# Raw queries and keys in a ring of five half buffers, and a 28th resident weight quarter

## The chip, the cores and the metric

The kernel runs on one core of a Trainium2 chip. The metric is the device time of one launch in microseconds (us), the median of several runs. Five engines work side by side: TensorE (PE, with its weight loads as PEld), VectorE (DVE), ScalarE (ACT), GpSimd (POOL) and SyncE (SP). SP issues all DMA transfers of this kernel, in one order written out in the program.

## What is computed

Attention with a decay for 8 batches of 8 heads (576 positions, 64 channels), and on its result a soft mixture of 8 experts:

```python
scores = scale * np.matmul(q, k.transpose(0, 1, 3, 2))
cum = np.cumsum(np.log(np.clip(f, 0.0001, 1.0)), axis=-1)
scores = np.where(causal, -1000000000.0, scores + cum[:, :, :, None] - cum[:, :, None, :])
attn = softmax(scores)                    # 64 heads, 576 x 576
x = (attn @ v)                            # then as 4608 x 512
logits = x @ phi                          # 32 slots, 4 for each expert
slot_input = softmax(logits, over tokens).T @ x
h = relu(slot_input[e] @ w1[e]); slot_out[e] = h @ w2[e]     # 8 experts, 512 x 1024 and 1024 x 512
out = softmax(logits, over slots) @ slot_out
```

## The kernel before

The 64 heads are worked off in 32 pairs; `g` is a pair, `h0 = 2g` and `h1 = 2g+1` are its heads. One pass of the loop over `g` (L699 on) does for pair `g` the scores (`s2`, L262), their exponentials (`expo`, on ACT, L282), the causal blanking (`causal`, on POOL: one L290 and two L293 for a head), and the product with the values (`s3`, 25 matmuls of the program for a head, L310). For the pairs ahead it does the score maxima (`s1` on PE, `tops` on DVE); those of pair `g+1` are turned into a row and sent with a small DMA (`mrows`, `YA<-mr`, L260), for which the first `s2` of the next pass waits. The values of a head are normed by `norm` on DVE (L325 to L330), and the normed tiles `X` are turned on PE by `px` (L337), for the logits of the experts.

Queries and keys come as fp32 (`load_qk`, `RAW<-in_qk`, L166: both heads of a pair in one transfer of 576 KB) and are split into two parts. ACT rounds them (`round_k` L175 into `WA`, `round_q` L180 into `YA`). Two DMAs on SP copy the rounded parts to the other half of the partitions (`dup_q` L195, `YB<-YA`, and `dup_k` L191, `WB<-WA`, 288 KB each for a pair). POOL subtracts the rounded from the raw: `low_k(i)` (L201) reads raw keys and the copy in `WB`, `low_q(i)` (L206) raw queries and `YA`. So a raw buffer is free when ACT has rounded and POOL has subtracted. There are three of them, `RAW[0]` to `RAW[2]`, one for a pair.

The expert weights are 64 quarters of 512 KB. In the loop, passes 4 to 30 each load one into a tile of its own (`wload`, `w<-in_w`, L120): 27 resident ones. The others go into tiles that the attention leaves (`wstream`): `RAW[2]`, then `RAW[0]` and two tiles `p2` at the end of pass 29, `RAW[1]`, `p0` and three `p1` at the end of pass 30, later `PTS`, `V`, `X`, and at last 20 of the resident tiles again. After the loop come the last logits, the two expert layers (`mlp1`, L907, and `mlp2`, L945) and the output in blocks (L1018, L1019), staged in the three raw buffers, `p2` and `p0`.

Nothing is scheduled by a planner: each engine does its instructions in the order of the program, and waits in place where an operand is not ready. The order in which each `s3` reads the columns of the probabilities `PT` is fixed by `VALUES` (L66): the 8th and the 9th of its 25 matmuls are the first that read columns which L293 blanks.

Of the kernel before, what the change touches and what calls it, by code (L numbers as in the profile page):

```python
# [7 lines left out]
F32 = mybir.dt.float32  # L8
# [19 lines left out]
TOP = (97, 66, 66)  # L28
NRES = 27
NQ = 8 * NE  # L30
QW = 1024
DEFER = 4
# [36 lines left out]
def attn_softmoe(ctx: ExitStack, tc: tile.TileContext, qk, v, f, phi, w1, w2, cst, out):  # L69
# [23 lines left out]
    for n, m in enumerate((1, 0, 2)):  # L93
        YA[m] = fr[n].tile([P, 2, 640], F32R, name=f"YA{m}")
        WA[m] = fr[n].tile([P, 2 * S], F32R, name=f"WA{m}")
        if m < 2:
            YB[m] = fr[n].tile([P, 2, S], F32R, name=f"YB{m}")
            WB[m] = fr[n].tile([P, 2 * S], F32R, name=f"WB{m}")
    RAW = [per.tile([P, 2, S], F32, name=f"RAW{i}") for i in range(3)]
    PTS = per.tile([P, 3200], F32, name="PTS")  # L100
    PT = [PTS[:, 1600 * i : 1600 * i + 1600] for i in range(2)]
    X = [per.tile([P, NBLK, 256], F32, name=f"X{i}") for i in range(3)]
    XT = [per.tile([P, S], F32, name=f"XT{i}") for i in range(NPAIR)]
    V = per.tile([P, 2, NBLK, 130], F32, name="V")
    EX = per.tile([P, 256], F32, name="EX")
    LD = const.tile([P, NBLK, NS], F32, name="LD")

    LG = const.tile([P, 256], F32, name="LG")
    fin = const.tile([P, 8], F32, name="fin")
# [36 lines left out]
    def pair(g):  # L146
        return 0 <= g < NG
# [14 lines left out]

    def load_qk(g):
        if pair(g) and ("r", g) not in st:
            st["r", g] = RAW[g % 3]
            nc.sync.dma_start(RAW[g % 3], qk[g])  # L166

    def load_v(g):
        if pair(g):
            nc.sync.dma_start(V[:, g % 2], v[g])  # L170

    def round_k(g, *hs):
        if pair(g):
            for h in hs or range(2):
                nc.scalar.copy(WA[g % 3][0:64, S * h : S * h + S], RAW[g % 3][64:128, h])  # L175

    def round_q(g, *hs):
        if pair(g):
            for h in hs or range(2):
                nc.scalar.copy(YA[g % 3][0:64, h, 64:640], RAW[g % 3][0:64, h])  # L180

# [11 lines left out]
    def dup_q(g, h0=0, h1=2):  # L193
        if pair(g):
            nc.sync.dma_start(YB[g % 2][0:64, h0:h1].bitcast(F32), YA[g % 3][0:64, h0:h1, 64:640].bitcast(F32))  # L195

    def low_k(i):
        if head(i):
            g, h = divmod(i, 2)
            t = WB[g % 2][:, S * h : S * h + S]  # L200
            nc.gpsimd.tensor_tensor(t[0:64], RAW[g % 3][64:128, h], t[64:128].bitcast(F32), op=ALU.subtract)  # L201

    def low_q(i):
        if head(i):
            g, h = divmod(i, 2)
            nc.gpsimd.tensor_tensor(YB[g % 2][64:128, h], RAW[g % 3][0:64, h], YA[g % 3][0:64, h, 64:640].bitcast(F32), op=ALU.subtract)  # L206

# [893 lines left out]
```

## Time and profile before

| | |
|---|---|
| median of 3 runs | 393.2 us (392.66 to 393.69) |
| profiled execution, own time | 395.0 us |
| its span (first to last instruction) | 393.2 us |
| TensorE busy | 372.6 us, 95% of the span |
| VectorE, ScalarE, GpSimd busy | 280.5, 260.1, 252.4 us |
| granted TensorE clock, mean | 0.985 |

Times in all rows are counted from the span's start. In a timeline row, the first number is the start and the second the duration, in us, of `xN` instructions in a row; in brackets stands the idle time before them and what ended it, where there was some. TensorE's records are finer than the program: a head's 25 matmuls of `s3` are 50 records. SP's rows are the issues of DMAs; the data moves later.

### The profile page before, as it was taken

What the parts mean: (1) busy time and instruction counts of PE and PEld (TensorE: products, weight loads), DVE (VectorE), ACT (ScalarE), POOL (GpSimd) and SP (SyncE); (2) the same over time, 40 slices, a digit from 0 to 9 for tenths busy, and PEclk for the clock granted to TensorE, in tenths of its full rate; (3) what the DMA queues carried; (4) which work ended last, traced back from release to release, by engine and by line L of the source; (5) the groups of instructions that cost most, each with busy time, mean ns of one, the idle gap of its engine ahead of it and who ended that gap; (6) DMA issues with size and microseconds to landing.
All of it is one profiled execution on the core that took longest, in us unless ns stands there. A gap on an engine that the chain in (4) does not pass through costs nothing.

```text
span 393.2 us, 15013 instructions
## 1 busy us (share of the span) xinstructions
PE 372.6 (95%) x5827; PEld 329.7 (84%) x5827; DVE 280.5 (71%) x1074; ACT 260.1 (66%) x664; POOL 252.4 (64%) x349
## 2 busy tenths in 40 slices
PE   7999999999999999999999999999999989999860
PEld 7889999999999999999999999999999986544630
DVE  7878887878787877797879787878787534441770
ACT  8859776867786778676868686868686552021650
POOL 4797887878787878787878787878787821100000
PEclk9999999999999999999999999999999999999995
DMA  6865768677867777777777777777777989999798
GB/s 205 214 157 160 219 170 275 190 221 211 240 190 230 212 215 210 215 204 217 210 213 212 210 212 211 212 213 211 211 215 205 306 291 330 390 408 370 262 364 320
DMA packets 34343, 93.71 MB, mean 238 GB/s; under 512 B 4266, under 2 KB 8288, under 8 KB 34272
## 3 DMA queue, kind: packets, MB, share of 16 engines
q1 hardware_dynamic: 34272, 92.75, 76.1%
q8 instruction: 46, 0.75, 0.8%
q14 instruction: 25, 0.20, 0.2%
HBM read 63.93 MB, written 9.73 MB: 187 GB/s over the span
## 4 chain that ended last, share of the span: by engine, by line
PE 83%; DMA 10%; DVE 2%; ACT 2%; issue 1%; DVEq 0%; SPq 0%; ACTq 0%
PE pv L310 25%; PE ring L275 14%; PE s L222 13%; PE ring L276 13%; DMA w<-in_w 6%; PE pv L337 4%; PE lg L373 3%; DMA out<-RAW 2%; PE more L907 2%; PE ds L457 2%; DMA YA<-mr 1%; PE ring L493 1%; PE pv L248 1%; DMA PTS<-in_f 1%; ACT PTS L282 1%
## 5 line engine op out<-in xcount | busy, mean ns | idle before, releaser
L282 ACT ACTIVATE PTS<-ring 128x320 f32<-128x320 f32 (+2 forms) x256 | 119.8, 513 | 65.3 <-PE ring L276 39.2
L275 PE MATMUL ring<-YA,WA 67*128 67x320 f32 (+9 forms) x384 | 121.9, 330 | 1.2 <-DMA YA<-mr 1.2
L238 DVE CUSTOM_DVE_ANT_0 s<-s,mask 128x320 f32<-128x320 f32 (+3 forms) x256 | 109.1, 442 | 5.4 <-PE s L222 0.9
L276 PE MATMUL ring<-YB,WB 128*128 128x320 f32 (+4 forms) x384 | 110.7, 296 | 0.0
L310 PE MATMUL pv<-V,PTS 128*64 128x65 f32 x3200 | 104.3, 223 | 0.7 <-ACT mr L257 0.7
L310 PEld LDWEIGHTS pv<-V,PTS 128*64 128x64 f32 x3200 | 99.6, 137 | 3.4 <-ACT mr L257 1.2
L222 PE MATMUL s<-WA,YA 66*128 66x288 f32 (+9 forms) x384 | 98.5, 312 | 0.5 <-ACT YA L180 0.2
L201 POOL TENSOR_TENSOR WB<-RAW,WB 64x576 fp32r<-64x576 f32 x64 | 90.3, 1411 | 11.2 <-ACT YA L180 5.3
L206 POOL TENSOR_TENSOR YB<-RAW,YA 64x576 fp32r<-64x576 f32 x64 | 89.5, 1417 | 2.5
L275 PEld LDWEIGHTS ring<-YA,WA 67*128 67x128 f32 (+3 forms) x384 | 69.7, 183 | 6.9 <-issue 2.1
L276 PEld LDWEIGHTS ring<-YB,WB 128*128 128x128 f32 (+1 forms) x384 | 69.9, 182 | 0.0
L222 PEld LDWEIGHTS s<-WA,YA 66*128 66x128 f32 (+1 forms) x384 | 62.9, 190 | 7.1 <-ACT PTS L282 1.4
L293 POOL TENSOR_SCALAR_AFFINE_SELECT PTS<-PTS 128x128 f32<-128x128 f32 (+1 forms) x128 | 31.3, 265 | 25.7 <-ACT PTS L282 23.8
L238 DVE DVE_READ_ACCUMULATOR2_ANT MT<- 128x1 f32 x310 | 44.1, 142 | 0.0
L290 POOL TENSOR_SCALAR_AFFINE_SELECT PTS<-PTS 128x384 f32<-128x384 f32 x64 | 33.3, 520 | 15.6 <-ACT PTS L282 11.7
L337 PE MATMUL pv<-cs,X 128*128 128x128 f32 x155 | 42.0, 276 | 0.0
L238 DVE CUSTOM_DVE_ANT_0 s<-s,mask,MT 128x288 f32<-128x288 f32 x62 | 32.6, 526 | 11.4 <-PE s L222 2.4
L175 ACT CAST WA<-RAW 64x576 fp32r<-64x576 f32 x64 | 40.1, 669 | 0.9
L180 ACT CAST YA<-RAW 64x576 fp32r<-64x576 f32 x63 | 39.5, 670 | 0.4
L325 DVE TENSOR_SCALAR rl<-pv 128x5 f32<-128x5 f32 x64 | 10.5, 164 | 35.9 <-PE pv L310 35.3
L330 DVE TENSOR_TENSOR X<-pv,rl 128x320 f32<-128x320 f32 (+1 forms) x65 | 31.5, 486 | 2.4 <-DMA w<-in_w 0.3
L361 ACT COPY XT<-pv 128x128 f32<-128x128 f32 (+1 forms) x124 | 28.6, 292 | 0.0
(210 smaller groups left out, 371.7 us busy)
## 6 DMA issues: line engine op xcount, KB each, us to landing
w<-in_w SPq DMA_DIRECT2D x47, 512.0 KB
RAW<-in_qk SPq DMA_DIRECT2D x31, 576.0 KB
V<-in_v SPq DMA_DIRECT2D x32, 325.0 KB
YB<-YA SPq DMA_DIRECT2D x30, 288.0 KB
WB<-WA SPq DMA_DIRECT2D x30, 288.0 KB
p<-in_w SPq DMA_DIRECT2D x6, 512.0 KB
out<-RAW SPq DMA_DIRECT2D x6, 512.0 KB
out<-p SPq DMA_DIRECT2D x5, 512.0 KB
```

The lines of the kernel that those rows point to most:

```text
L175: nc.scalar.copy(WA[g % 3][0:64, S * h : S * h + S], RAW[g % 3][64:128, h])
L180: nc.scalar.copy(YA[g % 3][0:64, h, 64:640], RAW[g % 3][0:64, h])
L201: nc.gpsimd.tensor_tensor(t[0:64], RAW[g % 3][64:128, h], t[64:128].bitcast(F32), op=ALU.subtract)
L206: nc.gpsimd.tensor_tensor(YB[g % 2][64:128, h], RAW[g % 3][0:64, h], YA[g % 3][0:64, h, 64:640].bitcast(F32), op=ALU.subtract)
L222: nc.tensor.matmul(t[:, o : o + w], ya[0:m, h, 128 * blk : 128 * blk + 128], wa[0:m, j0 : j0 + w], start=True, stop=True)
L238: nc.vector.tensor_tensor_reduce(out=t[:, o : o + w], in0=t[:, o : o + w], in1=mask[:, m0 : m0 + w], scale=1.0, scalar=top if n == 3 else ...
L275: nc.tensor.matmul(o, wa[0:m, j0 : j0 + n], ya[0:m, h, 64 + i0 : 64 + i0 + w], start=True, stop=False)
L276: nc.tensor.matmul(o, wb[:, j0 : j0 + n], yb[:, h, i0 : i0 + w], start=False, stop=True)
L282: nc.scalar.activation(PT[i % 2][:, SEG_O[bank] : SEG_O[bank] + at], t[:, 0:at], AF.Exp, scale=0.125)
L290: nc.gpsimd.affine_select(d3, d3, pattern=[[0, 3], [1, 128]], compare_op=ALU.is_ge, fill=0.0, base=0, channel_multiplier=-1)
L310: nc.tensor.matmul(o[64 * u : 64 * u + 64, t, :], PT[i % 2][:, at : at + 64], V[:, g % 2, c, 65 * h : 65 * h + 65], start=(c == 0), stop=( ...
L337: nc.tensor.transpose(pm[:, 0:128], x[:, t, 128 * (p % 2) : 128 * (p % 2) + 128], ident)
```

## The change

- The raw queries and keys stand in one tile of five half buffers, one for a head: `raw(i)` is half `i % 5`. `load_qk(g, h)` loads one head (288 KB), so a pair takes two transfers, and the second of pair `g+3` goes into the half of head `h0+2`.
- In each pass POOL does `low_q(h0+2)` and `low_k(h0+2)` at the start, `low_q(h1+2)` after `causal(h0)`, and `low_k(h1+2)` at the end as before. Before, both `low_q` stood at the start and `low_k(h0+2)` after `causal(h0)`. SP issues the first half load before the value load, the second behind it and then the resident quarter.
- `dup_k` is issued ahead of `dup_q` in the loop.
- 28 resident quarters: one in each of the passes 4 to 28, and a second one in passes 18, 22 and 26 (`TWICE`); none in 29 to 31.
- Of the raw tile two pieces are taken for streamed quarters: the first behind both `p2` at the end of pass 29, the second behind `p0` and `p1` at the end of pass 30. The load at the end of pass 28 is gone. The third stage tile for the output is the 28th resident quarter.
- `LG` is 194 columns wide, not 256, and the scratch for dynamic DMAs is 128, not 1024.

```diff
-NRES = 27
+NRES = 28
+TWICE = {18: 2, 22: 2, 26: 2, 29: 0, 30: 0, 31: 0}
...
-    RAW = [per.tile([P, 2, S], F32, name=f"RAW{i}") for i in range(3)]
+    RAW = per.tile([P, 5, S], F32, name="RAW")
...
-    def load_qk(g):
-        if pair(g) and ("r", g) not in st:
-            st["r", g] = RAW[g % 3]
-            nc.sync.dma_start(RAW[g % 3], qk[g])
+    def raw(i):
+        return RAW[:, i % 5]
+
+    def load_qk(g, *hs):
+        if pair(g):
+            for h in hs or range(2):
+                nc.sync.dma_start(raw(2 * g + h), qk[g][:, h])
...
+    resident = iter(range(NRES))
     for g in range(1, NG):
...
-        if g < 4:
-            load_v(g + 1)
-            load_qk(g + 3)
-        else:
-            load_qk(g + 3)
-            load_v(g + 1)
-            if g - 4 < NRES:
-                wload(g - 4)
+        load_qk(g + 3, 0)
+        load_v(g + 1)
         if w == 1:
             weigh(b)
         low_q(h0 + 2)
-        low_q(h1 + 2)
+        low_k(h0 + 2)
+        load_qk(g + 3, 1)
+        for _ in range(TWICE.get(g, 1) if g >= 4 else 0):
+            wload(next(resident))
...
         causal(h0)
-        low_k(h0 + 2)
+        low_q(h1 + 2)
...
         load_cum(g + 3)
+        dup_k(g + 2)
         dup_q(g + 2)
-        dup_k(g + 2)
         if g == 29:
...
-            wstream(RAW[30 % 3], *p2)
+            wstream(*p2, RW[:, 0:QW])
...
-            wstream(RAW[31 % 3], *p0, *p1)
+            wstream(*p0, *p1, RW[:, 2 * S : 2 * S + QW])
...
-        if g == 28:
-            wstream(RAW[29 % 3])
...
-    stage = [t.rearrange("p a b -> p (a b)") for t in RAW] + p2 + p0
+    stage = [RW[:, 0:QW], RW[:, 2 * S : 2 * S + QW], quarter[NRES - 1]] + p2 + p0
```

On POOL, in the first pass of the loop (`g = 1`), the order before is, from `low_q(3)` on (`YB` and `WB` with a tile's number behind the underscore; a row of L293 128x64 is the second of a head):

```order
L206 TENSOR_TENSOR YB1_87<-RAW1_96,YA1_85 64x576
L206 TENSOR_TENSOR YB0_91<-RAW2_97,YA2_93 64x576 x2
L290 AFFINE_SELECT PTS_98<-PTS_98 128x3x128
L293 AFFINE_SELECT PTS_98<-PTS_98 128x128
L293 AFFINE_SELECT PTS_98<-PTS_98 128x64
L201 TENSOR_TENSOR WB0_92<-RAW2_97,WB0_92 64x576
L290 AFFINE_SELECT PTS_98<-PTS_98 128x3x128
```

and now, with the same instructions at L212 (`low_q`), L207 (`low_k`), L296 and L299 (`causal`):

```order
L212 TENSOR_TENSOR YB1_87<-RAW_95,YA1_85 64x576
L212 TENSOR_TENSOR YB0_91<-RAW_95,YA2_93 64x576
L207 TENSOR_TENSOR WB0_92<-RAW_95,WB0_92 64x576
L296 AFFINE_SELECT PTS_96<-PTS_96 128x3x128
L299 AFFINE_SELECT PTS_96<-PTS_96 128x128
L299 AFFINE_SELECT PTS_96<-PTS_96 128x64
L212 TENSOR_TENSOR YB0_91<-RAW_95,YA2_93 64x576
L296 AFFINE_SELECT PTS_96<-PTS_96 128x3x128
```

`low_k(4)` has moved from behind the causal blanking of head 2 to ahead of it, and `low_q(5)` the other way.

On SP, at the end of the loop, the order before is, from the copies of pass 29 on:

```order
L195 DMA YB1_87<-YA1_85 64x2x576
L191 DMA WB1_88<-WA1_86 64x1152
L120 DMA RAW0_95<-in_w1 128x1024
L120 DMA p2_0_5334<-in_w1 128x1024
L120 DMA p2_1_5335<-in_w1 128x1024
L170 DMA V_106<-in_v 128x650
L120 DMA w26_142<-in_w1 128x1024
L260 DMA YA1_85<-mr31_0_5473 1x10x128
L120 DMA RAW1_96<-in_w1 128x1024
L120 DMA p0_0_5495<-in_w2 128x1024
```

and now (`mr31` is the row of maxima of pair 31):

```order
L197 DMA WB1_88<-WA1_86 64x1152
L201 DMA YB1_87<-YA1_85 64x2x576
L123 DMA p2_0_5365<-in_w1 128x1024
L123 DMA p2_1_5366<-in_w1 128x1024
L123 DMA RAW_95<-in_w1 128x1024
L176 DMA V_104<-in_v 128x650
L266 DMA YA1_85<-mr31_0_5503 1x10x128
L123 DMA p0_0_5525<-in_w2 128x1024
```

The resident quarter that stood between the value load and the row of maxima is no longer there; it is issued in an earlier pass.

## Rows read from the trace of the kernel before

**Rows 1.** The page's first part: busy time, share of the span and number of instructions of TensorE and the others.

```profile
PE 372.6 (95%) x5827; PEld 329.7 (84%) x5827; DVE 280.5 (71%) x1074; ACT 260.1 (66%) x664; POOL 252.4 (64%) x349
```

**Rows 2.** The view by stretches: length, then busy time and instructions of PE, PEld, DVE, ACT and POOL, the granted clock of TensorE, the busy share of the DMA engines, and GB/s moved.

```profile
100.00:200.00 100.00, 99.93 (x1721) 93.53 (x1718) 78.28 (x312) 75.28 (x196) 79.11 (x105) 1.00 0.73 211
...
340.00:350.00 10.00, 9.74 (x155) 5.18 (x147) 5.49 (x21) 2.69 (x8) 1.25 (x4) 1.00 1.03 409
350.00:360.00 10.00, 10.00 (x134) 4.20 (x122) 1.62 (x4) 1.00 (x3) 0.00 (x0) 1.00 1.03 408
```

**Rows 3.** Timeline of POOL in the first pass: `low_q(3)` to `low_q(5)`, `causal(2)`, `low_k(4)`, `causal(3)`, `low_k(5)`.

```profile
24.83 4.17 POOL L206 TENSOR_TENSOR YB<-RAW,YA 64x576 fp32r<-64x576 f32 x3
29.33 0.52 POOL L290 TENSOR_SCALAR_AFFINE_SELECT PTS<-PTS 128x384 f32<-128x384 f32 x1 [0.33 <-ACT PTS L282]
31.15 0.49 POOL L293 TENSOR_SCALAR_AFFINE_SELECT PTS<-PTS 128x128 f32<-128x128 f32 x2 [1.30 <-ACT PTS L282]
31.79 1.42 POOL L201 TENSOR_TENSOR WB<-RAW,WB 64x576 fp32r<-64x576 f32 x1
33.28 0.52 POOL L290 TENSOR_SCALAR_AFFINE_SELECT PTS<-PTS 128x384 f32<-128x384 f32 x1
33.98 0.49 POOL L293 TENSOR_SCALAR_AFFINE_SELECT PTS<-PTS 128x128 f32<-128x128 f32 x2 [0.18 <-ACT PTS L282]
34.55 1.42 POOL L201 TENSOR_TENSOR WB<-RAW,WB 64x576 fp32r<-64x576 f32 x1
```

**Rows 4.** Timeline of PE in the same pass: `s3(2)` and `s3(3)`.

```profile
33.15 3.25 PE L310 MATMUL pv<-V,PTS 128*64 128x65 f32 x100
```

**Rows 5.** Timeline of SP: the issues of `dup_q(2)` and `dup_k(2)`.

```profile
25.60 0.72 SPq L195 DMA_DIRECT2D YB<-YA  x1
26.37 0.60 SPq L191 DMA_DIRECT2D WB<-WA  x1
```

**Rows 6.** The view by stretches (columns as in rows 2) while those two copies move.

```profile
27.00:28.00 1.00, 1.00 (x13) 0.89 (x8) 0.89 (x7) 0.06 (x1) 1.00 (x2) 1.00 1.00 191
28.00:29.00 1.00, 1.00 (x9) 1.00 (x9) 0.85 (x3) 1.00 (x3) 0.99 (x1) 1.00 1.12 222
29.00:30.00 1.00, 1.00 (x10) 0.97 (x10) 0.97 (x5) 0.95 (x3) 0.52 (x1) 1.00 0.86 176
```

**Rows 7.** Timeline of POOL in passes 20 and 21: instructions that follow each other without a wait.

```profile
213.08 0.49 POOL L293 TENSOR_SCALAR_AFFINE_SELECT PTS<-PTS 128x128 f32<-128x128 f32 x2 [0.73 <-ACT PTS L282]
213.65 1.42 POOL L201 TENSOR_TENSOR WB<-RAW,WB 64x576 fp32r<-64x576 f32 x1
...
223.24 0.52 POOL L290 TENSOR_SCALAR_AFFINE_SELECT PTS<-PTS 128x384 f32<-128x384 f32 x1
223.71 0.49 POOL L293 TENSOR_SCALAR_AFFINE_SELECT PTS<-PTS 128x128 f32<-128x128 f32 x2
224.28 1.41 POOL L201 TENSOR_TENSOR WB<-RAW,WB 64x576 fp32r<-64x576 f32 x1
```

**Rows 8.** Timeline of SP at the end of the loop: issues of streamed quarters, of the last values, of the last resident quarter (L120, w), of the row of maxima of pair 31 (L260).

```profile
305.81 0.34 SPq L120 DMA_DIRECT2D RAW<-in_w  x1
306.20 1.36 SPq L120 DMA_DIRECT2D p<-in_w  x2
307.66 0.38 SPq L170 DMA_DIRECT2D V<-in_v  x1
308.08 0.59 SPq L120 DMA_DIRECT2D w<-in_w  x1
311.72 0.79 SPq L260 DMA_DIRECT2D YA<-mr  x1
314.74 0.34 SPq L120 DMA_DIRECT2D RAW<-in_w  x1
...
322.21 0.33 SPq L120 DMA_DIRECT2D PTS<-in_w  x1
```

**Rows 9.** Timeline of PE there: `s3(60)` and `s3(61)`, the first `s2` of pair 31, the first `px` of pair 30.

```profile
311.75 3.25 PE L310 MATMUL pv<-V,PTS 128*64 128x65 f32 x100 [0.24 <-ACT mr L257]
316.19 0.47 PE L275 MATMUL ring<-YA,WA 67*128 67x448 f32 x1 [1.19 <-DMA YA<-mr]
...
317.01 0.27 PE L337 MATMUL pv<-cs,X 128*128 128x128 f32 x1
```

**Rows 10.** Timeline of DVE there: the last step of `norm(61)`.

```profile
315.46 0.49 DVE L330 TENSOR_TENSOR X<-pv,rl 128x320 f32<-128x320 f32 x1
```

**Rows 11.** The chain of work that ended last, in order of time (start, duration, what).

```profile
311.72 4.42 DMA YA<-mr
...
351.07 11.58 DMA w<-in_w
```

**Rows 12.** The view by stretches (columns as in rows 2) for the microsecond in which PE waits there.

```profile
315.00:316.00 1.00, 0.00 (x0) 0.00 (x0) 0.89 (x4) 0.00 (x0) 0.00 (x0) 1.00 0.55 82
```

**Rows 13.** Timeline of SP in pass 21, one in which POOL's first step waits for the logits: the resident quarter and the row of maxima.

```profile
219.77 0.55 SPq L120 DMA_DIRECT2D w<-in_w  x1
...
224.87 0.79 SPq L260 DMA_DIRECT2D YA<-mr  x1
```

**Rows 14.** Timeline of PE in pass 21: both `s3`.

```profile
225.37 3.25 PE L310 MATMUL pv<-V,PTS 128*64 128x65 f32 x100
```

**Rows 15.** Timeline of ACT in pass 21: both halves of `round_k`.

```profile
226.02 1.24 ACT L175 CAST WA<-RAW 64x576 fp32r<-64x576 f32 x2
```

More of the change, by code (lines that the diff above doesn't have):

```diff
@@ L103, in attn_softmoe @@
     XT = [per.tile([P, S], F32, name=f"XT{i}") for i in range(NPAIR)]
+    RW = RAW.rearrange("p n s -> p (n s)")
     V = per.tile([P, 2, NBLK, 130], F32, name="V")
@@ L106, in attn_softmoe @@
     LD = const.tile([P, NBLK, NS], F32, name="LD")
-    LG = const.tile([P, 256], F32, name="LG")
+    LG = const.tile([P, 194], F32, name="LG")
     fin = const.tile([P, 8], F32, name="fin")
@@ L174, in round_k @@
             for h in hs or range(2):
-                nc.scalar.copy(WA[g % 3][0:64, S * h : S * h + S], RAW[g % 3][64:128, h])
+                nc.scalar.copy(WA[g % 3][0:64, S * h : S * h + S], raw(2 * g + h)[64:128])
     def round_q(g, *hs):
@@ L179, in round_q @@
             for h in hs or range(2):
-                nc.scalar.copy(YA[g % 3][0:64, h, 64:640], RAW[g % 3][0:64, h])
+                nc.scalar.copy(YA[g % 3][0:64, h, 64:640], raw(2 * g + h)[0:64])
     def load_cum(g):
@@ L200, in low_k @@
             t = WB[g % 2][:, S * h : S * h + S]
-            nc.gpsimd.tensor_tensor(t[0:64], RAW[g % 3][64:128, h], t[64:128].bitcast(F32), op=ALU.subtract)
+            nc.gpsimd.tensor_tensor(t[0:64], raw(i)[64:128], t[64:128].bitcast(F32), op=ALU.subtract)
     def low_q(i):
@@ L205, in low_q @@
             g, h = divmod(i, 2)
-            nc.gpsimd.tensor_tensor(YB[g % 2][64:128, h], RAW[g % 3][0:64, h], YA[g % 3][0:64, h, 64:640].bitcast(F32), op=ALU.subtract)
+            nc.gpsimd.tensor_tensor(YB[g % 2][64:128, h], raw(i)[0:64], YA[g % 3][0:64, h, 64:640].bitcast(F32), op=ALU.subtract)
     TOPS = ((0, 0, 2, 0, 320), (0, 320, 1, 0, 192), (1, 0, 4, 0, 288), (2, 0, 4, 288, 288), (3, 0, 3, 0, 448), (3, 448, 0, 0, 64))
@@ L499, in attn_softmoe @@
     fy = WB[1][:, 0:640].bitcast(F32)
-    st["r", 0] = RAW[0]
     nc.sync.dma_start(fx, f)
-    for h in range(2):
-        nc.sync.dma_start(RAW[0][:, h], qk[0][:, h])
+    load_qk(0)
     nc.sync.dma_start(mask, cst[:, 258:706])
@@ L522, in attn_softmoe @@
     nc.gpsimd.memset(YA[0][0:64, :, 0:64].bitcast(F32), 0.0)
-    nc.gpsimd.memset(LG[:, 128:256], -1.0e30)
+    nc.gpsimd.memset(LG[:, 128:194], -1.0e30)
     nc.gpsimd.memset(EX[:, 192:256], 0.0)
@@ L555, in attn_softmoe @@
     nc.scalar.activation(fin[:, 0:1], ones[:, 0:1], AF.Exp)
-    load_qk(2)
+    load_qk(2, 0)
     load_v(0)
@@ L599, in attn_softmoe @@
     dup_q(1, 0, 1)
+    load_qk(2, 1)
     both(0, 0)
@@ L604, in attn_softmoe @@
     both(0, 2)
-    nc.vector.tensor_copy(YA[1][0:64, 1, 64:640], RAW[1][0:64, 1])
+    nc.vector.tensor_copy(YA[1][0:64, 1, 64:640], raw(3)[0:64])
     warm(2, cs)
@@ L615, in attn_softmoe @@
     load_cum(2)
-    load_qk(3)
+    load_qk(3, 0)
     first(2, 2)
@@ L630, in attn_softmoe @@
     nc.sync.dma_start(mk, cst[:, 706:714])
+    load_qk(3, 1)
     first(3, 1)
@@ L1092 @@
     arrays = {n: np.ascontiguousarray(a) for n, a in arrays.items()}
-    nc = bacc.Bacc("TRN2", target_bir_lowering=False, num_devices=1, dynamic_dma_scratch_size=1024)
+    nc = bacc.Bacc("TRN2", target_bir_lowering=False, num_devices=1, dynamic_dma_scratch_size=128)
     args = [nc.dram_tensor(n, a.shape, mybir.dt.from_np(a.dtype), kind="ExternalInput").ap() for n, a in arrays.items()]
```

## The prediction

> **What bounds the kernel now.** I read the page's first part first, then stretches, then the waits in the places where TensorE is not full. TensorE is busy for 95% of the span [rows 1]. The stretches say where: in the middle of the attention loop it is busy 99.93 of 100 us at full granted clock, while POOL, DVE and ACT have a fifth or more to spare [rows 2]. So in the loop nothing that another engine or a transfer does costs anything until TensorE has to stop for it; and whatever stops it there is never made up, because there is no idle time later in which to catch up. After the loop it is different: from 340 to 360 us the DMA engines are full (share 1.03, 408 to 409 GB/s) [rows 2], and the chain that ended last runs over a weight load that took 11.58 us to land [rows 11]. That stretch is bound by transfers, and it begins when the attention's last tiles come free, that is, by TensorE's progress.
>
> So the reader should look for two things: places in the loop where the change makes TensorE stop, and places before the DMA-bound stretch where it takes a stop away. There is one such place before, at 315 us: TensorE idles 1.19 us for the row of maxima of pair 31 [rows 9], and that small transfer took 4.42 us from issue to landing [rows 11]. Its queue explains that: ahead of it stand three streamed quarters, one value load and one resident quarter, issued between 305.81 and 308.67 us [rows 8].
>
> **The change, part by part.**
>
> *The resident quarter in front of the last row of maxima.* Now no resident quarter is issued in pass 30. Of what stood ahead of the row, 512 KB = 0.524 MB are gone; at 409 GB/s [rows 2] that is 1.28 us. The row landed at 311.72 + 4.42 = 316.14 and would land at 314.86. The products before it end at 311.75 + 3.25 = 315.00 [rows 9], so the wait of 1.19 us goes. What is late next: `px` of pair 30 stands 0.82 us behind the first `s2` (317.01 against 316.19 [rows 9]), so it would come at 315.82, but it reads the tile that `norm(61)` finishes at 315.46 + 0.49 = 315.95 [rows 10]. It goes at about 316.05, so of 1.19 us some 0.95 are left. Bounds: nothing, if the row still lands last because of the other transfers ahead of it, and 1.2 us in full.
>
> *One more load in the loop, one fewer behind it.* The two loads of passes 29 and 30 and that at the end of pass 28 become the second loads of passes 18, 22 and 26 and a resident tile. From `PTS` on (322.21 us [rows 8]) both versions have the same 28 quarters to bring, each into a tile that TensorE has to leave first. So I cost this at nothing beyond the 0.95 us: the transfers behind 322 us start by TensorE's clock and all come earlier by as much as TensorE does.
>
> *`low_k(h0+2)` ahead of `causal(h0)`.* This is the edit with a price. `low_k` reads the copy that `dup_k` brings, so POOL may now wait for a DMA, and behind it in POOL's order stand the causal blanking of both heads, which the 8th and 9th matmul of each `s3` wait for. In the steady loop `dup_k` is now issued first, and POOL has slack: in pass 20, `causal(h0)` waits 0.73 us for ACT anyway [rows 7]. I cost it at nothing there. In the first pass the two copies still go out in the old order, `dup_q(2)` at 25.60 and `dup_k(2)` at 26.37 [rows 5]. When does the second one land? Together they are 0.590 MB, and the windows from 27 to 30 us move 0.191 + 0.222 + 0.176 = 0.589 MB [rows 6]: not before 30.0. Not after 31.79, when `low_k(4)` starts in the kernel before [rows 3]. In that bracket I take 31.7: POOL's gap ahead of `low_k(4)` is 31.79 - 31.64 = 0.15 us [rows 3], while without a wait it is 213.65 - 213.57 = 0.08, and 224.28 - 224.20 = 0.08 [rows 7]. So it was already waiting for the copy, hidden by the blanking that stood ahead.
>
> With that, `low_k(4)` stays at 31.79 to 33.21 and everything that stood ahead of it must come behind. L290 of head 2 at 33.28; L293 0.47 later as in rows 7, to 34.24; `low_q(5)` 34.32 to 35.73 (4.17 / 3 = 1.39 each [rows 3]); L290 of head 3 at 35.80, L293 to 36.76. TensorE's two `s3` are 100 records in 3.25 us [rows 4], 32.5 ns each, two records a matmul; the 9th matmul is 16 records in. For head 2 it stands at 33.15 + 0.52 = 33.67 and waits to 34.3. For head 3 it stood at 33.15 + 1.62 + 0.52 = 35.29 and now goes at 36.8: TensorE is 1.5 us late in all, and never catches up. I price a stop at its length alone: from 315 to 316 us TensorE did nothing, and its granted clock stayed at 1.00 [rows 12]. If the copy landed at 30.0, `low_k(4)` would run to 31.5, L293 of head 3 would end at 35.1, ahead of 35.29, and the price would be nothing. So between 0 and 1.5, and I take 1.5, by the gap.
>
> The Trainium skill ("DMA: Bandwidth & Descriptors", section "Anatomy of one DMA — SWDGE (gpsimd) path") gives a transfer about 2.0 us plus its bytes at 436 GB/s; that is its fit for transfers issued by GpSimd, and these are issued by SP. By that estimate `dup_k(2)` would land by 29.7 us, even behind the other copy, TensorE would not stop in the first pass, and the sum would be 392.2 instead. The trace speaks against that rate here, at some 196 GB/s in rows 6, so it stays a rival.
>
> *Half loads and their waits.* Each pass issues one DMA more (SP has idle time), the bytes are the same, and the second half waits for `low_k(h0+2)`. Queued behind it on SP is the resident quarter, and then the row of maxima. The tightest passes are those in which POOL's first step waits for the logits: in pass 21 `low_k` would end when L290 now starts, some 223.25 us [rows 7], so half load and quarter (0.295 + 0.524 MB) are issued by 224.2, still before the row at 224.87 [rows 13], and need 2.0 us at 409 GB/s plus their start. The row must land by the end of `s3`, 225.37 + 3.25 = 228.62 [rows 14]. It fits with about a microsecond to spare, and the half load must land before ACT casts its half, 0.62 us behind 226.02 [rows 15], which is closer. I cost this at nothing; if the cover is gone, it recurs in seven passes.
>
> *The rest* (`LG`, the scratch, the stage tiles, the changed order of loads before the loop) lies beside other work; nothing for it, within 0.2 us.
>
> **The sum.** -0.95 + 1.5 = +0.55 us, made against the profiled execution (span 393.2, own time 395.0, so 1.8 us lie around the span and stay). The median of the runs is 393.2, 1.8 below the profiled one; the difference carries over to 393.75, so 393.8 us.
>
> **Rivals.**
>
> 1. *The copy lands early and the first pass costs next to nothing.* For it: its bytes are through by about 30.0 [rows 6]. Against it: the 0.15 us gap. Then only the gain at 315 us is left: 392.0 to 392.3, say 392.1.
> 2. *The DMA-bound end itself gets shorter by a transfer.* If transfers left over from 314.74 us still hold up the `PTS` load at 322.21 [rows 8], the quarter taken out gives up to 1.28 us more on top, with part of the first pass's stop: 393.2 - 0.95 - 1.28 + 0.75 = 391.7. For it: the row at 311.72 shows a queue still full then. Against it: the waits behind 322 us are for TensorE's tiles.
> 3. *The late resident quarter holds up other things in the loop.* In the passes with logits (seven of them) the second half is asked for 5.5 us later than the whole pair was, and the quarter 4 us later than at 219.77. From the point where the half lands more than about 0.6 us behind 226.02 [rows 15], or the row behind 228.62 [rows 14], TensorE stops in each. At 0.3 us each that is 2.1 us on top: 393.75 + 2.1 = 395.9, slower.
> 4. *The wait at 315 us stays.* If the quarters ahead of the row still pile up, since both `p2` go out a little sooner, there is no gain and the first pass's 1.5 us remain: 394.7.
>
> **How the numbers follow.** Forecast (first pass stops, wait at 315 us goes) 0.45, with a range of its own from 393.0 to 394.6; rival 1 0.20; rival 2 0.14; rival 3 0.14; rival 4 0.07. What a measurement of this kernel can tell from no change is 0.3%, that is 1.2 us: below 392.0 is faster, above 394.4 slower. Faster: nearly all of rival 2 and under half of rival 1, 0.21. Slower: rival 3, most of rival 4 and the upper edge of the forecast, 0.25. The rest, 0.54, within. The range from 391.6 to 395.2 leaves out the lower half of rival 2 and most of rival 3.
>
> **What would show it.** In the changed profile the timeline of PE around 33 to 37 us: two stops inside `s3`, for POOL, of about 0.6 and 0.9 us, and the first `s2` of pass 2 at about 37.8 instead of 36.3; on POOL `low_k(4)` still near 31.8 with idle time ahead of it that ended with a DMA. At the end, no idle time of PE for `YA<-mr`; `px` behind `norm(61)`; the last loads and outputs shifted as one. In between the loop should be as full as in rows 2. I am wrong if PE runs through the first `s3` without a stop (rival 1), if the loop shows waits for `YA<-mr` or ACT's casts wait for `RAW<-in_qk` in passes 5, 9, 13 and so on (rival 3), or if the time from the `PTS` load to the last weight shrinks (rival 2).

## The result, and the profile after

The changed kernel takes 395.38 us (median of 18 runs, beside 393.76 us for 18 runs of the kernel before): ratio 1.0058, 95% interval 1.0035 to 1.0080, some 2.3 us slower where 0.55 was forecast. (The ratio is not that of the two medians, which lie 1.6 us apart: the changed kernel's times spread further upwards.) The median of 395.38 us is 0.2 above the forecast's range; by the ratio, on the 393.2 us that the prediction started from, it is 395.5 us, 0.3 above it. The execution profiled with that result was disturbed (587.6 us, TensorE at a clock of 0.56 throughout), and so was e6's below, so the rows here are of a second measurement of the changed kernel, called e1: 395.42 us beside 393.97, ratio 1.0055 (1.0034 to 1.0077), span 394.4.

The page's first part hardly moves against [rows 1]. TensorE is busy as long as before; the loss is idle time, spread thin:

```profile
PE 372.9 (95%) x5827; PEld 329.4 (84%) x5827; DVE 280.9 (71%) x1074; ACT 260.3 (66%) x664; POOL 253.6 (64%) x349
```

Where the idle time is, the timeline of PE tells (in brackets the idle time and what ended it). The first pass, which was one row before [rows 4]:

```profile
33.36 0.68 PE L316 MATMUL pv<-V,PTS 128*64 128x65 f32 x14
34.23 1.93 PE L316 MATMUL pv<-V,PTS 128*64 128x65 f32 x50 [0.19 <-POOL PTS L299]
36.77 1.46 PE L316 MATMUL pv<-V,PTS 128*64 128x65 f32 x36 [0.61 <-POOL PTS L299]
38.16 0.47 PE L281 MATMUL ring<-YA,WA 67*128 67x448 f32 x1
```

and POOL beside it (L207 is `low_k(4)`, L299 the blanking that TensorE waits for):

```profile
31.93 1.41 POOL L207 TENSOR_TENSOR WB<-RAW,WB 64x576 fp32r<-64x576 f32 x1 [4.16 <-DMA WB<-WA]
...
33.89 0.49 POOL L299 TENSOR_SCALAR_AFFINE_SELECT PTS<-PTS 128x128 f32<-128x128 f32 x2
...
36.43 0.49 POOL L299 TENSOR_SCALAR_AFFINE_SELECT PTS<-PTS 128x128 f32<-128x128 f32 x2
```

This is the forecast's picture: `low_k(4)` waits for the copy until 31.93 (forecast 31.79), both blankings come late, TensorE stops twice, and the first `s2` of pass 2 stands at 38.16. The idle times in brackets add up to 0.80 us only, but ends of matmuls are modelled, and the rows around a stop are drawn long. The honest measure is from row to row: `s3(2)` to that `s2` is 4.80 us, and 3.17 in e3 below, which has no stop: 1.63 us lost, where 1.5 was forecast.

The end of the loop (`s3(60)` and the first `px` of pair 30; no row between them has a wait), which answers to [rows 9]:

```profile
314.33 3.25 PE L316 MATMUL pv<-V,PTS 128*64 128x65 f32 x100 [0.24 <-ACT mr L263]
...
318.67 0.30 PE L343 MATMUL pv<-cs,X 128*128 128x128 f32 x1 [0.19 <-DVE lg L818]
```

The wait of 1.19 us for the row of maxima is gone, and `px` comes 4.34 us behind `s3(60)`, not 5.26: 0.92 us gained, as forecast, and DVE's work behind `norm(61)` is what is late next. But `s3(60)` itself starts at 314.33, 2.58 us later than before. Of these, 0.21 were there ahead of the first pass's `s3` and 1.63 came in it. The rest came in the middle of the loop, which the forecast held to be as full as before. The waits of PE between 40 and 312 us (total, times, longest) have two rows that the kernel before has not:

```profile
PE ring L281 <- DMA YA<-mr: 0.8, 1, 0.8
PE ring L281 <- DMA WB<-WA: 0.2, 1, 0.2
```

In the timeline they are the first `s2` of passes 6 and 23:

```profile
75.90 0.47 PE L281 MATMUL ring<-YA,WA 98*128 98x448 f32 x1 [0.17 <-DMA WB<-WA]
...
241.71 0.36 PE L281 MATMUL ring<-YA,WA 67*128 67x448 f32 x1 [0.76 <-DMA YA<-mr]
```

Pass 5 is one with logits; pass 22 follows one (21) and asks for two resident quarters. SP's issues in the two passes:

```profile
69.95 0.33 SPq L172 DMA_DIRECT2D RAW<-in_qk  x1
70.33 1.12 SPq L123 DMA_DIRECT2D w<-in_w  x1
71.54 0.79 SPq L266 DMA_DIRECT2D YA<-mr  x1
...
233.17 0.33 SPq L172 DMA_DIRECT2D RAW<-in_qk  x1
233.55 0.90 SPq L123 DMA_DIRECT2D w<-in_w  x2
236.17 0.81 SPq L266 DMA_DIRECT2D YA<-mr  x1
```

In pass 5 the half load and the quarter go out 1.6 and 1.2 us ahead of the row, in pass 22 the half and two quarters 3.0 and 2.6 us; in pass 21 of the kernel before, the quarter went out 5.1 us ahead of it [rows 13]. In pass 23 TensorE starts 5.54 us after the row's issue, while the row at the end of the kernel before took 4.42 us with a full queue in front [rows 11]. The Trainium skill ("DMA: Bandwidth & Descriptors", section "Queues, rings and completion order") says that SP has one ring on each DMA engine and that each is consumed in ring order; the rows agree as far as they go: the row of 5 KB is late where many bytes were issued just ahead of it.

The bytes ahead are not all of it. The trace records single DMA packets, and the row's ten packets of 512 bytes can be told by their size. In pass 22 nine of them had started by 239.12 us and the tenth at 240.41, just as a packet of instructions (16 KB, 239.32 to 240.42 us) ended. Had the tenth come with the ninth, the row would have been there 1.29 us sooner, more than the stop of 0.76 us. Over the profiles of e1, e3, e4 and e7 TensorE stops five times for the row, and in four of them its last packet starts within 0.1 us of the end of an instruction packet (in e4's pass 22, 242.59 and 242.61). The kernel before has such stragglers too (pass 18: the last packet at 198.19, the one ahead of it at 197.12), but there the row has slack to spare. So the late loads use up the slack, and an instruction packet can then make the stop. Which DMA engine a packet ran on the trace does not tell, and no run moved the instruction packets.

So two steps of the forecast came true, and something was added that it had priced at nothing. One execution cannot tell how much: the profiles below have these stops at different passes and of different lengths. The experiments ask for the parts one by one.

### The profile page after: what moved, and what is told of

Read it like the earlier page. It is cut to its first block, busy times and chain, and to the rows that moved or that the text cites. A ratio compares the mean times of both kernels' runs of the same rounds, so it can differ in the third digit from the quotient of the medians.

```text
span 587.6 us, 15100 instructions
## 1 busy us (share of the span) xinstructions
PE 575.4 (98%) x5827; PEld 482.7 (82%) x5827; DVE 299.6 (51%) x1074; ACT 276.7 (47%) x664; POOL 253.6 (43%) x349
## 4 chain that ended last, share of the span: by engine, by line
PE 97%; DVE 1%; issue 0%; ACT 0%
PE pv L316 28%; PE ring L281 14%; PE ring L282 14%; PE s L228 13%; PE pv L343 5%; PE pv L947 4%; PE more L909 4%; PE lg L379 3%; PE ring L499 3%; PE ds L463 2%; PE ring L1020 1%; PE pv L254 1%; PE more L1020 0%; PE pv L695 0%; PE pv L1020 0%
## 5 line engine op out<-in xcount | busy, mean ns | idle before, releaser
L316 PE MATMUL pv<-V,PTS 128*64 128x65 f32 x3200 | 167.6, 283 | 0.2
L316 PEld LDWEIGHTS pv<-V,PTS 128*64 128x64 f32 x3200 | 160.8, 184 | 4.2 <-issue 2.3
L281 PE MATMUL ring<-YA,WA 67*128 67x320 f32 (+9 forms) x384 | 161.0, 430 | 0.0
L282 PE MATMUL ring<-YB,WB 128*128 128x320 f32 (+4 forms) x384 | 150.8, 399 | 0.0
L228 PE MATMUL s<-WA,YA 66*128 66x288 f32 (+9 forms) x384 | 137.9, 422 | 0.0
L228 PEld LDWEIGHTS s<-WA,YA 66*128 66x128 f32 (+1 forms) x384 | 86.5, 244 | 13.6 <-issue 1.9
L207 POOL TENSOR_TENSOR WB<-RAW,WB 64x576 fp32r<-64x576 f32 x64 | 89.9, 1404 | 17.2 <-DMA WB<-WA 12.5
L281 PEld LDWEIGHTS ring<-YA,WA 67*128 67x128 f32 (+3 forms) x384 | 84.9, 222 | 14.8 <-issue 6.8
L212 POOL TENSOR_TENSOR YB<-RAW,YA 64x576 fp32r<-64x576 f32 x64 | 90.2, 1411 | 5.0
L282 PEld LDWEIGHTS ring<-YB,WB 128*128 128x128 f32 (+1 forms) x384 | 89.5, 233 | 1.8
L296 POOL TENSOR_SCALAR_AFFINE_SELECT PTS<-PTS 128x384 f32<-128x384 f32 x64 | 33.5, 524 | 88.6 <-ACT PTS L288 76.1
L299 POOL TENSOR_SCALAR_AFFINE_SELECT PTS<-PTS 128x128 f32<-128x128 f32 (+1 forms) x128 | 31.4, 267 | 90.3 <-ACT PTS L288 89.1
L343 PE MATMUL pv<-cs,X 128*128 128x128 f32 x155 | 59.6, 391 | 0.0
L242 DVE TENSOR_REDUCE MT<-s 128x1 f32<-128x288 f32 x62 | 28.3, 456 | 13.4 <-PE s L228 11.6
```

What stands on the lines that cost most here:

```text
L207: nc.gpsimd.tensor_tensor(t[0:64], raw(i)[64:128], t[64:128].bitcast(F32), op=ALU.subtract)
L212: nc.gpsimd.tensor_tensor(YB[g % 2][64:128, h], raw(i)[0:64], YA[g % 3][0:64, h, 64:640].bitcast(F32), op=ALU.subtract)
L228: nc.tensor.matmul(t[:, o : o + w], ya[0:m, h, 128 * blk : 128 * blk + 128], wa[0:m, j0 : j0 + w], start=True, stop=True)
L281: nc.tensor.matmul(o, wa[0:m, j0 : j0 + n], ya[0:m, h, 64 + i0 : 64 + i0 + w], start=True, stop=False)
L282: nc.tensor.matmul(o, wb[:, j0 : j0 + n], yb[:, h, i0 : i0 + w], start=False, stop=True)
L296: nc.gpsimd.affine_select(d3, d3, pattern=[[0, 3], [1, 128]], compare_op=ALU.is_ge, fill=0.0, base=0, channel_multiplier=-1)
```

## The experiments

Each is compared with runs of the kernel before on the same chip, made beside it (their median is given as "beside").

**e1 and e2: both kernels again.**

> The changed kernel once more, for a profile at full clock. Theory A (the first pass of the loop stops TensorE behind low_k(4)): the first s2 of pass 2 starts about 1.5 us later than before, near 37.8 us, with two idle times inside s3 for POOL, and no other stop in the loop. Rival B (the half loads and the late resident quarter stop TensorE again and again): waits for YA<-mr or for ACT's casts in several of the passes 5 to 29, of 0.3 us and more. Both: 1.003 to 1.008 of the kernel before.

> The kernel before, unchanged, for a second profile of it. If the wait of 1.19 us for YA<-mr at 315 us belongs to this kernel, it is there again, between 0.8 and 1.4 us; if it was a matter of that one execution, it is under 0.3 us and the term of -0.95 us in the sum has nothing to take away. Time 1.000 within 0.3%.

e1 is given above. e2, the kernel before: 393.65 us beside 393.97, ratio 0.9993 (0.9978 to 1.0007), so this is what no change looks like. Its profile (span 391.8) has the wait at 316 us again:

```profile
311.71 3.25 PE L310 MATMUL pv<-V,PTS 128*64 128x65 f32 x100 [0.24 <-ACT mr L257]
316.11 0.47 PE L275 MATMUL ring<-YA,WA 67*128 67x448 f32 x1 [1.15 <-DMA YA<-mr]
```

**e3: the first two copies swapped** in the changed kernel, keys first, so that `low_k(4)` has its copy sooner.

```diff
+    dup_k(2)
     dup_q(2)
-    dup_k(2)
```

> The changed kernel with dup_k(2) issued ahead of dup_q(2) before the loop. Theory A: dup_k(2) lands about 1.5 us sooner, the stops in the first pass shrink from 1.5 to under 0.4 us, and the time is 1.0 to 1.5 us below the changed kernel. Rival B: no change beyond 0.3 us, since the first pass is one of many.

394.45 us beside 393.97, ratio 1.0019 (0.9999 to 1.0039). The first pass is whole again, POOL first, then PE:

```profile
28.79 1.41 POOL L207 TENSOR_TENSOR WB<-RAW,WB 64x576 fp32r<-64x576 f32 x1 [1.28 <-DMA WB<-WA]
```

```profile
33.11 3.25 PE L316 MATMUL pv<-V,PTS 128*64 128x65 f32 x100
36.28 0.47 PE L281 MATMUL ring<-YA,WA 67*128 67x448 f32 x1
```

The key copy ends `low_k`'s wait 3.1 us earlier when it is first in SP's order. So the forecast's cause of the first stop is shown: about 0.36% or 1.4 us of the loss are this one line. But by the forecast's sum what is left would be 0.95 us faster than before, and it is not.

**e4: the old POOL order in the first pass only** (`if g > 1` around the early `low_k` and the half load), the copies as changed.

> The changed kernel, but in pass 1 alone both low_q at the start and low_k(4) behind causal(2), as before, with the second half load behind it. Theory A: no stop in the first pass, 1.3 to 1.6 us below the changed kernel. Rival B: no change beyond 0.3 us.

394.84 us beside 393.97, ratio 1.0028 (1.0005 to 1.0050): like e3. Its profiled execution is one of its longer ones (span 396.2), with no stop in the first pass and two long ones in the same passes as e1's. The first:

```profile
75.49 0.47 PE L281 MATMUL ring<-YA,WA 98*128 98x448 f32 x1 [1.49 <-DMA YA<-mr]
```

and the stretches behind it (columns as in rows 2):

```profile
75.00:76.00 1.00, 0.51 (x2) 0.49 (x3) 0.07 (x1) 0.00 (x0) 0.00 (x0) 1.00 0.93 237
76.00:77.00 1.00, 1.00 (x7) 0.98 (x6) 0.51 (x2) 0.73 (x2) 0.43 (x1) 0.73 0.97 184
77.00:78.00 1.00, 1.00 (x6) 0.96 (x5) 0.54 (x2) 0.49 (x3) 0.97 (x1) 0.50 0.84 278
78.00:79.00 1.00, 1.00 (x7) 1.00 (x6) 0.67 (x3) 0.42 (x3) 0.52 (x1) 0.50 0.17 58
79.00:80.00 1.00, 1.00 (x8) 0.96 (x7) 0.31 (x2) 0.00 (x0) 0.00 (x0) 0.56 0.92 238
80.00:81.00 1.00, 1.00 (x9) 0.93 (x8) 0.96 (x5) 0.80 (x2) 0.14 (x1) 1.00 0.99 338
```

After 1.49 us without work the granted clock falls to 0.50, 1.2 GHz, for some 3 us, so this stop costs about 1.5 + (0.27 + 0.50 + 0.50 + 0.44) = 3.2 us. That is twice its length; the forecast had priced a stop at its length.

**e5, e6, e7: where the resident quarter stands.** My theory A was that the late quarter, in front of the row, makes the stops; B that the late half load or the order of the copies does; C that the tail gives nothing. All three carry e3's swap. e5 asks for the quarter ahead of `weigh(b)`:

```diff
         load_v(g + 1)
+        for _ in range(TWICE.get(g, 1) if g >= 4 else 0):
+            wload(next(resident))
         if w == 1:
             weigh(b)
         low_q(h0 + 2)
         low_k(h0 + 2)
         load_qk(g + 3, 1)
-        for _ in range(TWICE.get(g, 1) if g >= 4 else 0):
-            wload(next(resident))
```

e6 puts the same two lines behind `mrows(g + 1)`; e7 sets `TWICE = {30: 0, 31: 0}` and begins with pass 2, so that no pass asks for two.

> The first two copies swapped as in e3, and the resident quarter asked for ahead of POOL's steps and the second half load in each pass, as in the kernel before. Theory A (the late quarter stands in front of the row of maxima and makes TensorE stop in some passes with logits): no wait for YA<-mr of over 0.1 us in passes 5 to 30 but those behind a double quarter, and about 393.0 to 393.4 us, the kernel before less the 0.95 us of the tail. Theory B (the late half load or the changed order of the two copies makes the stops, the quarter's place does not matter): as e3, about 394.4 us. Theory C (the tail gives nothing in timed runs): about 394.0 us.

> The first two copies swapped as in e3, and the resident quarters asked for behind the row of maxima in each pass. Theory A: no stop for the row anywhere, about 393.0 us, unless the copies WB<-WA and YB<-YA, which now stand behind the quarter, come too late; then stops for WB<-WA of up to 1 us in several passes and over 395 us. Theory B: as e3, about 394.4 us.

> The first two copies swapped as in e3, and no pass asks for two quarters: passes 2 and 3 ask for one each instead. If the doubles in passes 18, 22 and 26 make most of the stops: 393.0 to 393.5 us, and no wait for YA<-mr at the start of pass 23. If the passes with logits make them: as e3, about 394.4 us, waits at the start of pass 6 or others that follow a pass with logits.

e5: 395.57 us beside 392.99, ratio 1.0058 (1.0031 to 1.0086). e6: 413.36, ratio 1.0479 (1.0437 to 1.0522). e7: 394.55, ratio 1.0037 (1.0016 to 1.0058). So theory A falls: an early quarter doesn't help, it rather hurts (e5 is above all three answers), and a quarter behind the row, where the two copies of keys and queries stand behind it, is far worse (where the 20 us arise was not seen). Where e5 loses, its waits of ACT between 40 and 312 us show: behind the early quarter the second half load comes late for ACT's cast, which waits for it 12 times, in all for 11.1 us; e1 and e7 have no such wait there.

```profile
ACT WA L181 <- DMA RAW<-in_qk: 11.1, 12, 3.6
```

The doubles are not most of the loss either: e7 is not below e3. It has no stop in passes 4 to 30 in its profile, but one where a quarter is new, at the start of pass 3:

```profile
46.98 0.47 PE L281 MATMUL ring<-YA,WA 98*128 98x448 f32 x1 [0.98 <-DMA YA<-mr]
```

**e8: the kernel before without the quarter in pass 30** (`TWICE = {18: 2, 30: 0, 31: 0}` in it), the tail's term alone.

> The kernel before with one edit: the resident quarter of pass 30 is asked for in pass 18, so none stands ahead of the last row of maxima. By the prediction's term: the 1.15 us wait at 316 us goes and about 393.0 us, ratio 0.9975. If the term was wrong: the wait stays, 394.0 us; if a second quarter in one pass is enough for a stop: the wait goes, another of about 1 us stands at the start of pass 19, 394.0 us.

393.10 us beside 392.99, ratio 0.9992 (0.9977 to 1.0006). The wait shrinks, but does not go:

```profile
315.71 0.47 PE L277 MATMUL ring<-YA,WA 67*128 67x448 f32 x1 [0.42 <-DMA YA<-mr]
```

It is 0.7 us shorter than in e2, and the interval, -0.9 to +0.2 us, holds that. The term has the right sign and place; alone it is smaller than 0.95, as the other transfers in front still hold the row: its last packet starts at 314.99 us, right behind packets of 2600 bytes, the value load's size.

**e9 to e12: the small edits, one by one, in the kernel before.** Theory P: the smaller transfers cost; theory T: it is not what is loaded but when, the second half going out late. e9 splits each load of a pair in two, issued together; e10 takes the changed order of POOL and of the copies; e11 the order of the copies in the loop alone; e12 the scratch alone.

```diff
-                nc.sync.dma_start(RAW[g % 3], qk[g])
+            for h in range(2):
+                nc.sync.dma_start(RAW[g % 3][:, h], qk[g][:, h])
```

> The kernel before with each pair's queries and keys asked for as two halves, one right behind the other, into the same full buffers. Theory P (the smaller pieces of 2304 bytes cost transfer time and make the loop's transfers late): stops for YA<-mr or WB<-WA in the loop, 394 to 395.5 us, scatter as wide as that of the changed kernel. Theory T (it is the late time of the second half, not its size): as before, within 0.3 us of it, and no stop in the loop.

> The kernel before with its full buffers and its early loads, but POOL's order and the order of the two copies as in the changed kernel (in the first pass's copies too). Theory T: as before, within 0.3 us. If POOL's order or that of the copies makes the stops: waits of TensorE for POOL, YA<-mr or WB<-WA in the loop, 394 to 395.5 us.

> The kernel before with only the order of the two copies in the loop turned (keys first). Theory T: as before, within 0.3 us. If this order makes the stops: YB<-YA lands about 1.5 us later, TensorE waits for low_q's tile, 394 us or more.

> The kernel before with only the scratch for descriptors cut from 1024 to 128 bytes. By the prediction (nothing for it): as before, within 0.3 us. If a smaller scratch holds up SP's issues: waits in SP's rows longer than before, 394 us or more.

Beside 393.01 us: e9 393.72, ratio 1.0020 (0.9999 to 1.0041); e10 394.09, 1.0014 (0.9998 to 1.0030); e11 393.87, 1.0007 (0.9992 to 1.0022); e12 394.56, 1.0026 (1.0015 to 1.0038). No profile of the four has a stop in the loop. e9 to e11 lie a little above no change, none of them clearly. The small scratch alone does lie clearly above; e15 takes it up again.

**e13 and e14: the same transfers, early and late.** e13 is the kernel before with all edits of order, sizes and quarters, but with its full buffers, so that both halves and the quarter can go out at the start of the pass. e14 adds one wait: SP must read one element of what `low_k(h0+2)` writes before it goes on. Theory U: the small edits add up.

```diff
         low_q(h0 + 2)
         low_k(h0 + 2)
+        if g >= 4:
+            if head(h0 + 2):
+                nc.sync.dma_start(gate, WB[(g + 1) % 2][0:1, 0:1].bitcast(F32))
+            load_h(g + 3, 1)
+            for _ in range(TWICE.get(g, 1)):
+                wload(next(resident))
```

> The kernel before with POOL's order, the order of the copies (in the first pass too), half loads and no resident quarter in passes 29 and 30 (two in passes 18 and 22), but full buffers, so that both halves and the quarter go out at the start of the pass. Theory T (the loop's stops come from the second half and the quarter going out late, close ahead of the row of maxima): no stop in the loop, about 393 us, at most 0.3 us above before. Theory U (the smaller edits add up, each with a few tenths): 394 us or more.

> As e13, with one thing more: from pass 4 on SP waits for low_k(h0+2) (by a transfer of one element from what it writes) before it asks for the second half and the quarter, as the ring of five makes it wait in the changed kernel. Theory T: stops of TensorE for YA<-mr or WB<-WA in the loop, wide scatter, 1 to 2.5 us above e13. Theory U: as e13, within 0.5 us.

Beside 393.56 us, e13 takes 393.26, ratio 0.9985 (0.9965 to 1.0005), and its waits of PE between 40 and 312 us have one row, which the kernel before has too:

```profile
PE pv L317 <- ACT mr L264: 0.2, 1, 0.2
```

e14 takes 399.89, ratio 1.0134 (1.0096 to 1.0173), and has, in the one profiled (its longest):

```profile
PE ring L283 <- DMA YA<-mr: 4.4, 5, 1.6
PE ring L283 <- DMA WB<-WA: 2.6, 4, 1.3
```

SP in pass 16, e13 first (quarter, row), then e14 (half, quarter, row):

```profile
172.65 0.42 SPq L122 DMA_DIRECT2D w<-in_w  x1
175.88 0.80 SPq L267 DMA_DIRECT2D YA<-mr  x1
```

```profile
177.53 0.36 SPq L174 DMA_DIRECT2D RAW<-in_qk  x1
177.96 0.53 SPq L123 DMA_DIRECT2D w<-in_w  x1
178.59 0.82 SPq L268 DMA_DIRECT2D YA<-mr  x1
```

The same bytes, 3.2 us ahead of the row in one and 0.6 in the other, decide between no stop and nine. So theory T holds for the stops, and U falls. For the price e14 is no measure: at some 5.9 us above e13 it is far over the 1 to 2.5 us that were expected, which I put down to the gate, a transfer of its own for which the half waits in every pass; that was not tried apart. (A rival, that SP's wait for the half holds up the issue of the row itself, falls: in e1 SP issues the row 0.02 to 0.04 us after ACT has made it, in every pass from 2 on, and in e14's loop at most 0.23 us after.)

**e15: the small scratch with the tiles where they were** (an unused tile of 896 bytes ahead of all others).

> As e12 (scratch of 128 bytes), with an unused tile of 896 bytes ahead of all others, so that every tile stands at the address that it has in the kernel before. If the size of the scratch cost the 0.26% of e12: as e12, about 1.0 us above before. If it was the addresses of the tiles: as before, within 0.3 us.

394.12 us beside 393.56, ratio 1.0010 (0.9986 to 1.0034): between the two answers. Why e12 is slower stays open.

**e16, e17, e18: the wait in front of the half load taken away.** In the passes with logits POOL stands at `weigh(b)` first. Pass 21 in e3, POOL and SP:

```profile
220.43 0.23 POOL L387 COPY EX<-LG 32x64 f32<-32x64 f32 x1 [2.29 <-ACT LG L386]
220.74 1.42 POOL L212 TENSOR_TENSOR YB<-RAW,YA 64x576 fp32r<-64x576 f32 x1
222.23 1.42 POOL L207 TENSOR_TENSOR WB<-RAW,WB 64x576 fp32r<-64x576 f32 x1
```

```profile
223.68 0.33 SPq L172 DMA_DIRECT2D RAW<-in_qk  x1
224.06 0.42 SPq L123 DMA_DIRECT2D w<-in_w  x1
225.23 0.80 SPq L266 DMA_DIRECT2D YA<-mr  x1
```

e16 is e3 with `weigh(b)` behind the loads; e17 has the quarter ahead of `low_q(h0+2)` as well; e18 is e16 with the first two copies in their old order.

```diff
-        if w == 1:
-            weigh(b)
         low_q(h0 + 2)
         low_k(h0 + 2)
         load_qk(g + 3, 1)
         for _ in range(TWICE.get(g, 1) if g >= 4 else 0):
             wload(next(resident))
+        if w == 1:
+            weigh(b)
```

> As e3 (the changed kernel with its first two copies swapped), with weigh(b) behind low_k(h0+2), the second half and the quarter, so that in the seven passes with logits POOL does not wait for the logits first and the half and the quarter go out some 4 us earlier. If the lateness in the passes with logits makes most of the stops: 393.2 us or less, no stop at the start of passes 6, 10, 14 and so on. If the other passes make them as well (the half goes out 2.5 to 3 us ahead of the row there): as e3, 0.5 us or more above before.

> As e16, and the quarter asked for ahead of low_q(h0+2), so that only the second half waits for POOL. If the bytes close ahead of the row decide: at or below e16, 393 us. If the second half alone, however early the quarter, makes the stops (e5 spoke for that): as e16 or above.

> The changed kernel with weigh(b) moved as in e16, the first two copies in their old order: the fourth corner of a square with the changed kernel, e3 and e16. If the stop in the first pass (about 1.2 to 1.5 us) and the lateness in the passes with logits (about 1.3 us) simply add: ratio to before of 1.002 to 1.003, about 1 us above before, the two stops in the first pass in the profile, none in passes 5 to 30. If the move of weigh(b) had only a lucky call in e16: as the changed kernel, 1.0055.

e16: 393.97 us beside 394.59, ratio 0.9987 (0.9969 to 1.0005). e17: 394.55 beside 394.59, ratio 1.0007 (0.9983 to 1.0031). e18: 394.52 beside 393.90, ratio 1.0027 (1.0007 to 1.0047); its profile has one of the two stops of the first pass (0.61 us) and no wait for a DMA in the loop. In e16's pass 5 the half and the quarter are 3.7 and 3.3 us ahead of the row (e1: 1.6 and 1.2), and its profile has no wait for a DMA in the loop:

```profile
66.50 0.33 SPq L172 DMA_DIRECT2D RAW<-in_qk  x1
66.88 0.42 SPq L123 DMA_DIRECT2D w<-in_w  x1
70.20 0.79 SPq L266 DMA_DIRECT2D YA<-mr  x1
```

e17 is not below e16, and its profile tells why an early quarter does not help there either: ACT waits for half loads for 10.5 us in all, and behind the longest wait (3.75 us) TensorE stops for ACT.

```profile
203.39 0.39 PE L281 MATMUL ring<-YA,WA 67*128 67x256 f32 x1 [1.05 <-ACT PTS L288]
```

With the changed kernel and e3, e16 and e18 make a square of ratios, each to the runs of the kernel before beside it:

| | copies in the old order | copies swapped |
|---|---|---|
| `weigh(b)` first | 1.0055 (e1) | 1.0019 (e3) |
| `weigh(b)` behind the loads | 1.0027 (e18) | 0.9987 (e16) |

The swap gives 0.36% in the upper row and 0.40% in the lower, 1.4 to 1.6 us; the move of `weigh(b)` gives 0.28% and 0.32%, 1.1 to 1.3 us. Each interval is some 0.2% to either side, and a difference of two is good to about 0.3% only; but each edit gives nearly the same in both places, so the two losses are separate as far as this can tell. The profiles do not show the second one at its size: in e1 only one of the passes with logits is followed by a stop (pass 5, 0.17 us), and the larger stop comes behind the two quarters of pass 22. It rests on timed runs. e16 keeps the 28th quarter and makes up all that the change had lost; that it beats the kernel before as well is not shown, and neither is it for e13.

## Why the prediction failed

By the square, the loss of 2.2 us is about +1.5 for the first pass, +1.2 for the late loads in the loop, and -0.5 for all the rest. Against the prediction's steps:

- *"`low_k(h0+2)` ahead of `causal(h0)`"*, +1.5 us: right in place, cause and size. (TensorE stops after 14 records, ahead of the 8th matmul and not the 9th, and 34.32 + 1.39 is 35.71, not 35.73; neither matters.) The 0.15 us gap ahead of `low_k(4)` had told when the copy lands (31.9, not 30.0): the operation that started a little later than others of its kind was waiting, though the view named no wait. By the Trainium skill's estimate quoted in the prediction, the copy would have been there at 29.7; the measurement decides against it. Rival 1 falls.
- *"The resident quarter in front of the last row of maxima"*, -0.95 us: 0.92 in e1's profile, from `s3(60)` to `px`. In timed runs the change's whole remainder is about -0.5 us (e16, -1.2 to +0.2), and the term alone -0.3 (e8). Right in mechanism; if it was off, then on the large side. Some of it can go again behind the loop: in the logits behind the loop (L379) TensorE stops for 0.21 us in e1, 0.26 in e5 and 0.81 in e18 with no releaser named, and in neither profile of the kernel before. Rival 4 falls. Rival 2 is not seen: e16, which would show it, gains less than the one term.
- *"Half loads and their waits. ... I cost this at nothing"*: this is the step that failed, and it held the warning itself ("if the cover is gone, it recurs in seven passes"). I compared issue times with a mean rate: 0.82 MB at 409 GB/s in 2.0 us, so the row would fit with about a microsecond to spare. But the row must wait for what stands in front of it however long that takes in this execution: in pass 22 of e1, with 1.34 MB in front, it was not there 5.5 us after its issue, 1.3 of them for one packet behind a packet of instructions. A microsecond of slack beside a wait that varies by more than that is not cover. In its place the runs showed a loss of about 1.2 us in the loop, the one that moving `weigh(b)` takes back. The mechanism was rival 3's, to which I had given 0.14. That its time of 393.75 + 2.1 = 395.9 us comes near the 395.5 is in part luck: it counted seven equal stops, where pass 29 asks for neither half nor quarter and e1's profile has one of the six others.
- *"I price a stop at its length alone"*, from one stop of 1.19 us at a clock of 1.00: right for the first pass, wrong for the stop of 1.49 us in e4, which cost about 3.2.
- *"The rest ... nothing for it, within 0.2 us"*: the small scratch alone measured +1.0 us in the kernel before (e12), and this could not be traced. In e16, which has the small scratch too, no loss of that size is left over.

## What to carry to other kernels

When a load is made to wait for an engine's step, look at what stands behind it in the same queue: here a row of 5 KB that TensorE needs each pass paid for 0.8 MB asked for a few us later, and moving an unrelated wait on POOL out of the way of that load took back about 1.2 us. Moving the other bulk load ahead of it did not help, since the load behind then came late for its own reader. Judge the slack of a transfer by its worst landing in the trace, not by bytes over a mean rate. And where one profile shows stops in other places than the next, take the price from many timed runs of a square of edits, not from one execution.

## What the runs showed of the hardware

- The granted clock does not follow the length of a stop alone: in e4 the 1.49 us stop at 75.49 was followed by a clock of 0.50, while a longer one in the same execution (1.92 us, until 244.05) was not:

```profile
243.00:244.00 1.00, 0.00 (x0) 0.19 (x1) 0.08 (x1) 0.00 (x0) 0.00 (x0) 1.00 0.96 308
...
245.00:246.00 1.00, 1.00 (x10) 0.99 (x9) 0.84 (x3) 0.89 (x3) 0.85 (x1) 1.00 0.14 43
```

- TensorE can stop for something that no operand explains. In e5 and in e16, at the same place of the program (`s3` of pass 26, after 81 records), the profile names no releaser, e5 first:

```profile
278.31 0.80 PE L316 MATMUL pv<-V,PTS 128*64 128x65 f32 x19 [0.91 <-issue]
```

```profile
277.75 0.80 PE L316 MATMUL pv<-V,PTS 128*64 128x65 f32 x19 [0.43 <-issue]
```

  In e5's window from 275 to 278.4 us the view of the DMA queues lists packets of instructions among the data, with the engines nearly full:

```profile
q1 hardware_dynamic: 270, 0.68, 82.6%
q8 instruction: 1, 0.02, 1.8%
```

  In e2, the kernel before, the same window has no such packet and TensorE no stop. The profiles of all runs but two (the changed kernel's first and e6) have seven such stops of TensorE, in e1, e5 (two), e14, e16, e17 and e18. In each, TensorE goes on 1.2 to 1.6 us after a 16 KB packet of instructions has ended (e5: 276.79 and 278.31). That instructions came late behind data would explain it; it was not tried.
